# Softmax of k with channels on partitions: maximum by free-axis reductions, subtraction as the bias of the exponential, 32x32 transposes in place

## Chip, cores and metric

The kernel runs on one core of a Trainium2 chip. The metric is the device time of one execution in microseconds (us), as the median of several runs; lower is better. All times below come from the runs, or from one execution that the hardware profiler recorded.

## What is computed

The inputs are eight images (b = 0 to 7) of eight heads, 576 tokens and 64 channels per head. Three blocks follow one another: linear attention, a gated block whose gate mixes tokens, and a gated convolution block.

```python
def _attn_ref(q, k, v):
    q_s = np.exp(q - np.max(q, axis=-1, keepdims=True))        # over channels
    q_s = q_s / (np.sum(q_s, axis=-1, keepdims=True) + 1e-09)
    k_s = np.exp(k - np.max(k, axis=2, keepdims=True))         # over tokens
    k_s = k_s / (np.sum(k_s, axis=2, keepdims=True) + 1e-09)
    kv = np.einsum('bhsd,bhse->bhde', k_s, v)
    return np.einsum('bhsd,bhde->bhse', q_s, kv)
...
    x = attn_out.transpose(0, 2, 1, 3).reshape(B, S, H * D)
    h = gelu_tanh(x @ w_in);  u, v = h[..., :512], h[..., 512:]
    v_s = np.einsum('ts,bsd->btd', w_sg, layernorm(v) * g_ln) + b_sg[None, :, None]
    x = x + (u * v_s) @ w_out
...
    h = np.maximum(x @ w_in2, 0.0)
    return (h * sigmoid(conv3(h, conv_w))) @ w_out2
```

The softmax of k runs over the tokens, separately for each head and channel: 512 maxima per image. Its denominator is not computed apart: v carries a column of ones, so that the matmul of k and v gives the sums too.

## The kernel before

Matmuls are done in three passes of fp32r operands split in a high and a low part (`mm3`, lines 61 to 64). The run has three stretches. Up to about 57 us the inputs land, image 0 goes through attention on a path of its own (functions `s_...`, lines 574 to 653), and the weights begin to be split into high and low parts (`Split`). Then the loop over images (lines 779 to 813) runs attention's remainder and the gated block; it ends near 600 us. The convolution block follows to the end.

In the loop, image b's gated block is a list of 29 groups of matmuls: four `hv` tiles of 128 tokens (and a tile of the leftover tokens of two images), then `hu`, `mx` and `wo` by turns. After each group, `attend` runs steps of other work that `PLAN` (lines 22 to 30) lists by letters: `k` is a step of the k stream, `q` of the q stream, `w` of the weight split, `s` of the mixing matrix's split. The k stream (`k_steps`, line 216) has eleven steps for each of images 1 to 7, and runs one to two images ahead of the gated block.

k of one image arrives with one DMA in the tile `kt`, 128 partitions by 2304. Tokens lie on partitions: block t of 512 columns holds tokens 128t to 128t+127 of all 512 channels; the last 256 columns hold the 64 leftover tokens, heads 0 to 3 on the lower 64 partitions and heads 4 to 7 on the upper ones. The steps are:

- `top`: VectorE takes the maximum over the four blocks and the leftover, down to 128 x 512 in the scratch tile `scr` (lines 221 to 224).
- `spread`: a 32x32 transpose (229), a reduction to 16 numbers per partition (230), exchanges between halves and neighbouring quarters of the partitions (`swap64`, `swap32`, lines 204 to 214), and a transpose that broadcasts the 512 maxima back over the partitions (235).
- `sub`: GpSimd subtracts them in six instructions (241 to 243).
- `ex`: ScalarE takes the exponential of all 2304 columns in one instruction (246).
- `left_max` to `left_tr`: q's 64 leftover tokens.
- `back_kv` twice: 80 small matmuls with 64 columns of `kt` as weights (368, 372), division by the sums, a split; the second then issues the loads of the next k and v. `xt_left` last.

GpSimd executes in the order of the program (`manual_schedule`). The other engines' order is set by a planner as the program is built: an instruction that is earlier in the program goes first among those that its model finds ready. Each engine then executes its own list strictly in order. What stands beside the k steps in those lists: `hv`'s Gelu on ScalarE (428) that frees a PSUM tile, its statistics on VectorE (432 to 436), and between them GpSimd's `pow` (435), a 128 x 1 instruction that `vnh` (444) and `lt` (453) wait for. The matmul groups take PSUM tiles from a pool of four (`mm_tile`). ScalarE loads a table whenever it goes from Gelu to exponential or back; a copy needs none.

Of the kernel before, what the change touches and what calls it, by code (L numbers as in the profile page):

```python
# [8 lines left out]
F32 = mybir.dt.float32  # L9
F32R = mybir.dt.float32r  # L10
U32 = mybir.dt.uint32
AF = mybir.ActivationFunctionType
ALU = mybir.AluOpType
# [23 lines left out]
def attn_gated_conv_kernel(ctx, tc, q, k, v, q0, k0, w_in, g_ln, w_sgT, b_sg, w_out, w_in2, conv_w, w_out2, out):  # L37
# [141 lines left out]
    at = es2.enter_context(tc.tile_pool(name="at", bufs=1, side="right", reuse_waits="tile"))  # L179

    kt = at.tile([128, 2304], F32, name="kt")
    vt = at.tile([128, 18, 2, 65], F32, name="vt")
    ql = [at.tile([128, 512], F32R, name=f"ql{c}") for c in range(4)]
    qlL = at.tile([128, 256], F32R, name="qlL")
# [29 lines left out]
                dve.tensor_copy(dst[32 * i:32 * i + 32], src[32 * j:32 * j + 32])  # L214

    def k_steps(b):
        m, mT, bc = scr[:, 0:512], scr[:, 512:1024], scr[:, 0:512]
        left = kt[:, 2048:2304]

        def top():  # L220
            E[CFG['kt'][min(b - 1, 3)]].tensor_tensor(scr, kt[:, 0:1024], kt[:, 1024:2048], ALU.max)
            dve.tensor_tensor(m, scr[:, 0:512], scr[:, 512:1024], ALU.max)
            dve.tensor_tensor(m[0:64, 0:256], m[0:64, 0:256], left[0:64], ALU.max)
            dve.tensor_tensor(m[64:128, 256:512], m[64:128, 256:512], left[64:128], ALU.max)

        def spread():
            r1 = at.tile([128, 16], F32, tag="r1", name="r1")
            r2 = at.tile([128, 16], F32, tag="r2", name="r2")
            dve.transpose(out=mT, in_=m)
            dve.tensor_reduce(r1, mT.rearrange("p (a b) -> p a b", b=32), axis=AX.X, op=ALU.max)  # L230
            swap64(r2, r1)
            dve.tensor_tensor(r1, r1, r2, ALU.max)
            swap32(r2, r1)
            dve.tensor_tensor(r1, r1, r2, ALU.max)
            dve.transpose(out=bc.rearrange("p (a b) -> p a b", b=32),
                          in_=r1.unsqueeze(2).to_broadcast([128, 16, 32]))

        def sub():
            for t in range(4):
                kc = kt[:, t * 512:t * 512 + 512]  # L240
                pool.tensor_tensor(kc, kc, bc, ALU.subtract)
            pool.tensor_tensor(left[0:64], left[0:64], bc[0:64, 0:256], ALU.subtract)
            pool.tensor_tensor(left[64:128], left[64:128], bc[64:128, 256:512], ALU.subtract)

        def ex():
            act.activation(kt, kt, AF.Exp)

        qv = qt[4].rearrange("p (j a) -> p j a", a=32)
        lm = at.tile([128, 8], F32, tag="lm", name="lm")
        lx = at.tile([128, 8], F32, tag="lx", name="lx")  # L250

        def left_max():
            dve.tensor_reduce(lm, qv, axis=AX.X, op=ALU.max)
            swap32(lx, lm, CFG['sl'][min(b - 1, 2)])
            dve.tensor_tensor(lm, lm, lx, ALU.max)
            pool.tensor_tensor(qv, qv, lm.unsqueeze(2).to_broadcast([128, 8, 32]), ALU.subtract)

        def left_exp():
            act.activation(qv, qv, AF.Exp)
            dve.tensor_reduce(lm, qv, axis=AX.X, op=ALU.add)  # L260

        def left_mul():
            swap32(lx, lm, CFG['sl'][min(b - 1, 2)])
            dve.scalar_tensor_tensor(lm, lm, 1e-9, lx, ALU.add, ALU.add)
            dve.reciprocal(lm, lm)
            pool.tensor_tensor(qv, qv, lm.unsqueeze(2).to_broadcast([128, 8, 32]), ALU.mult)

        def left_tr():
            t = at.tile([128, 256], F32, tag="qTL", name="qTL")
            dve.transpose(out=t, in_=qv.rearrange("p j a -> p (j a)"))  # L270
            qh[4] = at.tile([128, 256], F32R, tag="q4", name="q4")
            act.activation(qh[4], t, AF.Copy)
            dve.tensor_tensor(qlL, t, r32(qh[4]), ALU.subtract)

        return [top, spread, sub, ex, left_max, left_exp, left_mul, left_tr,
                lambda: back_kv(b, 0), lambda: back_kv(b, 1), lambda: xt_left(b)]

    def q_steps(b):
# [80 lines left out]
    def back_kv(b, c2):  # L359
        ps = mm_tile()  # L360
        for i in range(2):
            hp = c2 * 2 + i
            for t in range(5):
                for e in range(2):
                    o = ps[64 * e:64 * e + 64, i * 128:i * 128 + 65]
                    if t < 4:
                        c = t * 512 + hp * 128 + 64 * e
                        pe.matmul(o, kt[:, c:c + 64], vt[:, t * 4 + hp, e], start=(t == 0), stop=False)
                    else:
                        r = slice(0, 64) if hp < 2 else slice(64, 128)  # L370
                        c = 2048 + i * 128 + 64 * e
                        pe.matmul(o, kt[r, c:c + 64], vt[r, 16 + i, e], start=False, stop=True)
        pv = ps[:, 0:256].rearrange("p (c f) -> p c f", c=2)
        rt = at.tile([128, 2], F32, tag=f"rs{c2}", name=f"rs{c2}")
        kvf = scr[:, 512:768].rearrange("p (c f) -> p c f", c=4)
        dve.tensor_scalar(rt, pv[:, :, 64], 1e-9, None, ALU.add)
        dve.reciprocal(rt, rt)
        dve.tensor_tensor(kvf[:, 2 * c2:2 * c2 + 2], pv[:, :, 0:64], rt.unsqueeze(2).to_broadcast([128, 2, 64]), ALU.mult)
        if c2 == 0:
            return  # L380
        for e in range(2):
            r = slice(64 * e, 64 * e + 64)
            act.activation(kv_hi[r, :, r], kvf[r], AF.Copy)
        for e in range(2):
            r = slice(64 * e, 64 * e + 64)
            dve.tensor_tensor(kv_lo[r, :, r], kvf[r], r32(kv_hi[r, :, r]), ALU.subtract)
        if b + 1 < B:
            load_k(b + 1)
            load_v(b + 1)
# [192 lines left out]
    def s_kt(hp):  # L582
        ps = mm_tile()
        for t in range(4):
            o = hp * S + t * 128
            pe.transpose(ps[:, t * 128:t * 128 + 128], k0t[:, o:o + 128], ident)
        act.activation(kt[:, 0:2048].rearrange("p (t f) -> p t f", t=4)[:, :, hp * 128:hp * 128 + 128],
                       ps.rearrange("p (t f) -> p t f", t=4), AF.Copy)

    def s_ktl():  # L590
        ps = mm_tile()
# [347 lines left out]
def _layouts(i):  # L939
    import numpy as np  # L940

    def token_major(a):
        a = a.transpose(0, 2, 1, 3).reshape(-1, S, DM)
        main = a[:, :512].reshape(-1, 4, 128, DM).transpose(0, 2, 1, 3).reshape(-1, 128, 2048)
        left = a[:, 512:].reshape(-1, 64, 2, 256).transpose(0, 2, 1, 3).reshape(-1, 128, 256)
        return np.concatenate([main, left], axis=2)
# [4 lines left out]
    k0 = i["k"][0].transpose(0, 2, 1).reshape(4, 128, S).transpose(1, 0, 2)  # L951
    k0 = k0.reshape(128, 4 * S)
    conv = i["moe2_conv_w"].reshape(3, NFC, 128).transpose(2, 0, 1).reshape(128, 3 * NFC)
    r = {
        "q": q,
        "k": token_major(i["k"]),
        "v": token_major(i["v"]).reshape(B, 128, 18, 2, 64),
        "q0": token_major(i["q"][0:1])[0],
        "k0": k0,
# [28 lines left out]
```

## Time and profile before

| | |
|---|---|
| median of 3 runs | 1017.7 us (1016.02 to 1017.9) |
| span of the profiled execution, first to last instruction | 1016.5 us |
| TensorE (matmul) busy | 942.5 us, 93% |
| VectorE busy | 777.1 us, 76%, 1414 instructions |
| ScalarE busy | 459.6 us, 45%, 902 instructions |
| GpSimd busy | 433.5 us, 43%, 526 instructions |
| mean granted TensorE clock | 0.966 of full speed |

The time of the profiled execution itself is not given apart from its span; the median of the runs is 1.2 us above the span. In the rows, PE is TensorE, PEld its weight loads, DVE VectorE, ACT ScalarE, POOL GpSimd. A busy time counts instructions, not how well they use the engine; consecutive instructions of DVE and ACT overlap a little, so a sum of durations is slightly more than the time that passes. In a timeline, what stands in brackets is how long the engine had been idle and whose result it then waited for.

### The profile page before, as it was taken

The page shows a single profiled execution, that of the slowest core. Times are in us where ns is not written, and L with a number is a line of the kernel's source. Part 1 is how long each engine was busy: PE and PEld are TensorE (multiplying, and loading weights), DVE is VectorE, ACT ScalarE, POOL GpSimd, SP SyncE. Part 2 cuts the span into 40 slices and gives each one's busy share as a digit, 9 for nine tenths or more (in the row PEclk, how much of TensorE's full clock was granted, in tenths as well). Part 3 has the DMA queues.
Part 4 walks back from the last instruction along what each step waited for, and adds up shares of the span by engine and source line. Part 5 has one row for each costly group of instructions (what it writes and reads, how often), then busy time and mean ns, then how long its engine had stood idle before and what let it go on. Part 6 is the DMA issues. An engine that isn't in the chain of part 4 may idle for free.

```text
span 1016.5 us, 16164 instructions
## 1 busy us (share of the span) xinstructions
PE 942.5 (93%) x6144; PEld 851.9 (84%) x6144; DVE 777.1 (76%) x1414; ACT 459.6 (45%) x902; POOL 433.5 (43%) x526
## 2 busy tenths in 40 slices
PE   4777988999999999999988989799999999999998
PEld 3566968879889899898977989699999999989996
DVE  8999896898687777967898598977476757675663
ACT  6554635455546246463534245434343434343332
POOL 6378736556744376556576286611011101110000
PEclk9687997999999999999999998899999999999999
DMA  7721322151143212310222242112011201010001
GB/s 239 231 86 42 106 81 73 48 167 32 50 117 111 67 32 74 104 41 29 84 84 89 75 149 88 47 43 75 25 48 42 88 12 54 36 43 11 14 28 52
DMA packets 34564, 74.10 MB, mean 73 GB/s; under 512 B 3508, under 2 KB 14772, under 8 KB 32696
## 3 DMA queue, kind: packets, MB, share of 16 engines
q1 hardware_dynamic: 34488, 73.09, 22.8%
q8 instruction: 48, 0.79, 0.3%
q14 instruction: 28, 0.23, 0.1%
HBM read 54.20 MB, written 18.87 MB: 72 GB/s over the span
## 4 chain that ended last, share of the span: by engine, by line
PE 44%; DVE 10%; POOL 2%; ACT 2%; issue 2%; DMA 1%; POOLq 0%; DVEq 0%; ACTq 0%
PE mm L62 8%; PE mm L64 8%; PE mm L63 8%; PE acc L63 6%; PE acc L62 6%; PE acc L64 6%; DVE t L100 1%; DVE t L106 1%; DVE t L99 1%; POOL s L110 1%; DVE gl L498 1%; DVE x2s L519 1%; DVE s L109 1%; DMA s<-in_w_out 1%; ACT s L101 0%
## 5 line engine op out<-in xcount | busy, mean ns | idle before, releaser
L62 PE MATMUL mm<-xh,w2h 128*128 128x288 f32 x512 | 153.0, 299 | 3.9 <-ACT h L843 3.9
L64 PE MATMUL mm<-xh,w2l 128*128 128x288 f32 x512 | 152.6, 298 | 0.0
L63 PE MATMUL mm<-xl,w2h 128*128 128x288 f32 x512 | 152.4, 298 | 0.0
L62 PE MATMUL acc<-wAh,yh 128*128 128x512 f32 x256 | 101.5, 396 | 5.3 <-ACT yh L855 5.3
L62 PEld LDWEIGHTS mm<-xh,w2h 128*128 128x128 f32 x512 | 97.7, 191 | 7.2 <-ACT h L843 4.5
L63 PE MATMUL acc<-wAl,yh 128*128 128x512 f32 x256 | 101.9, 398 | 0.0
L63 PEld LDWEIGHTS mm<-xl,w2h 128*128 128x128 f32 x512 | 97.7, 191 | 2.5
L64 PE MATMUL acc<-wAh,yl 128*128 128x512 f32 x256 | 98.7, 395 | 0.0
L64 PEld LDWEIGHTS mm<-xh,w2l 128*128 128x128 f32 x512 | 97.8, 191 | 0.1
L853 ACT ACTIVATE cv<-cv 128x576 f32<-128x576 f32 x64 | 43.9, 685 | 115.9 <-DVE cv L847 115.8
L856 DVE TENSOR_TENSOR yl<-cv,yh 128x576 fp32r<-128x576 f32 x64 | 51.9, 811 | 52.4 <-ACT yh L855 52.4
L843 ACT ACTIVATE h<-mm 128x288 f32<-128x288 f32 x128 | 52.3, 411 | 80.4 <-PE mm L64 80.4
L62 PE MATMUL mm<-xh,wAh 128*128 128x288 f32 x256 | 78.0, 305 | 7.5 <-DVE u L493 4.0
L64 PE MATMUL mm<-sgh,vnl 128*128 128x288 f32 x256 | 77.2, 303 | 5.2 <-DVE rd L434 3.2
L62 PE MATMUL mm<-sgh,vnh 128*128 128x288 f32 x256 | 78.1, 306 | 3.9 <-ACT u L479 2.4
L520 POOL TENSOR_TENSOR x2s<-x2s,xl 128x288 f32<-128x288 f32 x64 | 55.6, 897 | 60.5 <-DVE x2s L519 48.1
L854 DVE TENSOR_TENSOR cv<-cv,h 128x576 f32<-128x576 f32 x64 | 48.8, 764 | 41.5 <-ACT cv L853 40.8
L63 PE MATMUL acc<-gl,wouth 128*128 128x288 f32 x256 | 73.4, 301 | 5.6 <-DVE gl L498 5.6
L64 PE MATMUL mm<-xh,wAl 128*128 128x288 f32 x256 | 77.6, 303 | 0.8 <-POOL wAl L119 0.7
L63 PE MATMUL mm<-xl,wAh 128*128 128x288 f32 x256 | 77.3, 302 | 0.0
L63 PE MATMUL mm<-sgl,vnh 128*128 128x288 f32 x256 | 77.0, 301 | 0.0
L295 POOL TENSOR_TENSOR q<-q,qm 128x512 f32<-128x512 f32 x56 | 61.1, 1121 | 36.1 <-PE mm L64 14.8
(245 smaller groups left out, 2728.4 us busy)
## 6 DMA issues: line engine op xcount, KB each, us to landing
vt<-in_v SPq DMA_DIRECT2D x8, 1152.0 KB, 10.1
x2d<-x2s SPq DMA_DIRECT2D x16, 576.0 KB, 3.3
out<-ot SPq DMA_DIRECT2D x32, 256.0 KB, 2.1
kt<-in_k SPq DMA_DIRECT2D x7, 1152.0 KB, 5.2
xf<-x2d SPq DMA_DIRECT2D x7, 1152.0 KB, 5.6
q<-in_q SPq DMA_DIRECT2D x28, 256.0 KB, 2.6
s<-in_w_in SPq DMA_DIRECT2D x16, 256.0 KB, 2.9
s<-in_w_out SPq DMA_DIRECT2D x16, 256.0 KB, 2.6
```

Source lines behind the costliest of these rows:

```text
L62: pe.matmul(ps, ah, bh, start=start, stop=False)
L63: pe.matmul(ps, ah, bl, start=False, stop=False)
L64: pe.matmul(ps, al, bh, start=False, stop=stop)
L99: dve.tensor_scalar(a.bitcast(U32), h, 3, 0x3FFFFFF8, ALU.logical_shift_left, ALU.bitwise_and)
L100: dve.scalar_tensor_tensor(a.bitcast(U32), h, 0xC0000000, a.bitcast(U32), ALU.bitwise_and, ALU.bitwise_or)
L106: dve.scalar_tensor_tensor(a, hf, GUARD * GUARD, a, ALU.is_ge, ALU.mult)
L295: pool.tensor_tensor(q3[c], q3[c], qm[:, cols(c)].unsqueeze(2).to_broadcast([128, 16, 32]), op)
L520: (dve if CFG['x2'][min(b, 2)] == 'd' else pool).tensor_tensor(x2s[:, m], x2s[:, m], r32(x_lo[b][:, m, cs]), ALU.add)
L843: act.activation(h[:, 1 + hf * HALF:1 + hf * HALF + HALF], ps, AF.Relu)
L853: act.activation(cv, cv, AF.Sigmoid)
L854: dve.tensor_tensor(cv, cv, h[:, 1:S + 1], ALU.mult)
L856: dve.tensor_tensor(yl, cv, r32(yh), ALU.subtract)
```

## The change

k arrives in another layout. Instead of tokens, 32 channels lie on a group of 32 partitions: partition 32g + r holds channel r (of the lower or upper half of a head's 64) for token quarter g of each block of 128, and the free axis runs over head, block, channel half and the quarter's 32 tokens. So each row of the tile belongs to one channel of a head, up to the four groups of partitions.

- `top` becomes four reductions of 128 x 512 and one of 128 x 256, with negated maxima.
- `spread` keeps the exchanges, now with minima, loses both transposes and the 512-wide reduction, gains two small minima with the leftover's, two ScalarE copies of 64 x 8, and one GpSimd addition of 128 x 256 (the leftover's subtraction).
- `sub` is gone; `ex` becomes 16 exponentials of 128 columns (four runs of 32), each with a bias read per partition, and one of 256.
- A new step `turn` transposes `kt` in place in 32x32 blocks: five VectorE instructions. After it tokens lie on partitions as before.
- The number of steps stays eleven; `PLAN` is unchanged. `back_kv` reads its weights at other columns, and `s_kt`, which writes image 0's k, makes two copies per head pair where it made one.

```diff
     def k_steps(b):
-        m, mT, bc = scr[:, 0:512], scr[:, 512:1024], scr[:, 0:512]
-        left = kt[:, 2048:2304]
+        k4 = kt[:, 0:2048].rearrange("p (h t e r) -> p h e t r", h=8, t=4, e=2)
+        left = kt[:, 2048:2304].rearrange("p (g r) -> p g r", r=32)
...
         def top():
-            E[CFG['kt'][min(b - 1, 3)]].tensor_tensor(scr, kt[:, 0:1024], kt[:, 1024:2048], ALU.max)
-            dve.tensor_tensor(m, scr[:, 0:512], scr[:, 512:1024], ALU.max)
-            dve.tensor_tensor(m[0:64, 0:256], m[0:64, 0:256], left[0:64], ALU.max)
-            dve.tensor_tensor(m[64:128, 256:512], m[64:128, 256:512], left[64:128], ALU.max)
+            for i in range(4):
+                dve.tensor_reduce(r1[:, 4 * i:4 * i + 4].rearrange("p (h e) -> p h e", h=2), k4[:, 2 * i:2 * i + 2],
+                                  axis=AX.XY, op=ALU.max, negate=True)
+            dve.tensor_reduce(lb, left, axis=AX.X, op=ALU.max, negate=True)
 
         def spread():
-            r1 = at.tile([128, 16], F32, tag="r1", name="r1")
-            r2 = at.tile([128, 16], F32, tag="r2", name="r2")
-            dve.transpose(out=mT, in_=m)
-            dve.tensor_reduce(r1, mT.rearrange("p (a b) -> p a b", b=32), axis=AX.X, op=ALU.max)
+            for e in range(2):
+                r = slice(64 * e, 64 * e + 64)
+                dve.tensor_tensor(r1[r, 8 * e:8 * e + 8], r1[r, 8 * e:8 * e + 8], lb[r], ALU.min)
             swap64(r2, r1)
-            dve.tensor_tensor(r1, r1, r2, ALU.max)
+            dve.tensor_tensor(r1, r1, r2, ALU.min)
             swap32(r2, r1)
-            dve.tensor_tensor(r1, r1, r2, ALU.max)
-            dve.transpose(out=bc.rearrange("p (a b) -> p a b", b=32),
-                          in_=r1.unsqueeze(2).to_broadcast([128, 16, 32]))
-
-        def sub():
+            dve.tensor_tensor(r1, r1, r2, ALU.min)
+            for e in range(2):
+                r = slice(64 * e, 64 * e + 64)
+                act.activation(lb[r], r1[r, 8 * e:8 * e + 8], AF.Copy)
+            pool.tensor_tensor(left, left, lb.unsqueeze(2).to_broadcast([128, 8, 32]), ALU.add)
+
+        def ex():
+            for g in range(16):
+                kg = k4[:, g // 2, g % 2]
+                act.activation(kg, kg, AF.Exp, bias=r1[:, g:g + 1])
+            act.activation(kt[:, 2048:2304], kt[:, 2048:2304], AF.Exp)
+
+        def turn():
             for t in range(4):
                 kc = kt[:, t * 512:t * 512 + 512]
-                pool.tensor_tensor(kc, kc, bc, ALU.subtract)
-            pool.tensor_tensor(left[0:64], left[0:64], bc[0:64, 0:256], ALU.subtract)
-            pool.tensor_tensor(left[64:128], left[64:128], bc[64:128, 256:512], ALU.subtract)
-
-        def ex():
-            act.activation(kt, kt, AF.Exp)
+                dve.transpose(out=kc, in_=kc)
+            dve.transpose(out=kt[:, 2048:2304], in_=kt[:, 2048:2304])
...
-        return [top, spread, sub, ex, left_max, left_exp, left_mul, left_tr,
+        return [top, spread, ex, turn, left_max, left_exp, left_mul, left_tr,
...
-                        c = t * 512 + hp * 128 + 64 * e
+                        c = (hp * 2 + e) * 256 + t * 64
...
-        act.activation(kt[:, 0:2048].rearrange("p (t f) -> p t f", t=4)[:, :, hp * 128:hp * 128 + 128],
-                       ps.rearrange("p (t f) -> p t f", t=4), AF.Copy)
+        for e in range(2):
+            act.activation(ktv[:, hp * 2 + e], ps.rearrange("p (t e d) -> p e t d", t=4, e=2)[:, e], AF.Copy)
```

## Rows read from the trace of the kernel before

**Rows 1.** Busy time per engine in stretches: stretch, length, busy (instructions), granted clock, DMA.

```profile
core 0: us, PE busy (x) PEld busy (x) DVE busy (x) ACT busy (x) POOL busy (x), PEclk, DMA share, GB/s
57.00:94.00 37.00, 22.95 (x105) 19.25 (x105) 36.75 (x45) 18.06 (x32) 29.60 (x22) 0.77 0.25 73
...
115.00:220.00 105.00, 94.59 (x709) 83.41 (x705) 89.58 (x189) 49.03 (x94) 62.66 (x62) 0.95 0.37 107
220.00:480.00 260.00, 254.38 (x1882) 234.54 (x1882) 202.39 (x438) 126.40 (x244) 147.28 (x144) 1.00 0.23 67
...
165.00:180.00 15.00, 14.02 (x112) 13.06 (x108) 12.48 (x33) 6.69 (x14) 5.65 (x6) 0.66 0.54 153
```

**Rows 2.** Timeline of TensorE, where it had been idle: start, duration, instruction, idle time.

```profile
93.10 0.61 PE L62 MATMUL mm<-xh,wAh 128*128 128x288 f32 x1 [2.99 <-DVE u L493]
...
163.73 0.69 PE L368 MATMUL mm<-vt,kt 128*64 128x65 f32 x16 [2.25 <-ACT kt L246]
167.78 1.13 PE L368 MATMUL mm<-vt,kt 128*64 128x65 f32 x16 [0.98 <-DVE u L493]
```

**Rows 3.** Sums over images 1 to 7: instructions on `scr`, then on `kt`.

```profile
sum 103.00, PE 0.00 PEld 0.00 DVE 42.31 ACT 0.00 POOL 0.00; mean PE 0.00 PEld 0.00 DVE 6.04 ACT 0.00 POOL 0.00
...
sum 81.00, PE 1.15 PEld 1.08 DVE 0.00 ACT 14.91 POOL 53.67; mean PE 0.16 PEld 0.15 DVE 0.00 ACT 2.13 POOL 7.67
```

**Rows 4.** VectorE by line and shape: count, busy us, mean ns of one.

```profile
L290 DVE TENSOR_REDUCE qm<-q 128x16 f32<-128x512 f32 x56 | 37.5, 675 | 13.6 <-ACT q L304 11.0 <-DMA q<-in_q 2.5
L316 DVE STREAM_TRANSPOSE qT<-q 128x512 f32<-128x512 f32 x28 | 19.5, 698 | 6.6 <-POOL q L295 3.9 <-POOL ql L320 2.6
...
L270 DVE STREAM_TRANSPOSE qTL<-q 128x256 f32<-128x256 f32 x7 | 3.1, 439 | 2.1 <-POOL q L266 1.9
L260 DVE TENSOR_REDUCE lm<-q 128x8 f32<-128x256 f32 x7 | 2.9, 413 | 6.0 <-ACT q L259 6.0
```

**Rows 5.** GpSimd by line and shape.

```profile
L241 POOL TENSOR_TENSOR kt<-kt,scr 128x512 f32<-128x512 f32 x28 | 40.8, 1488 | 7.4 <-issue 7.4
...
L256 POOL TENSOR_TENSOR q<-q,lm 128x256 f32<-128x256 f32 x7 | 5.0, 712 | 0.0
```

**Rows 6.** ScalarE by line and shape.

```profile
L212 ACT ACTIVATE lx<-lm 32x8 f32<-32x8 f32 x48 | 9.9, 206 | 6.2 <-DVE lm L253 4.0 <-DVE lm L260 1.4
...
L246 ACT ACT_TABLE_LOAD x7 | 9.0, 1283 | 0.1
...
L259 ACT ACTIVATE q<-q 128x256 f32<-128x256 f32 x7 | 2.9, 410 | 0.7 <-POOL q L256 0.6
```

**Rows 7.** Timeline of ScalarE: exponentials with a bias at the start, table loads later.

```profile
7.32 0.35 ACT L578 ACTIVATE scr<-k0t,sm 128x64 f32<-128x64 f32 x1
7.58 0.71 ACT L580 ACTIVATE k0t<-k0t,sm 128x512 f32<-128x512 f32 x1
8.19 0.62 ACT L599 ACTIVATE q0t<-q0t 128x512 f32<-128x512 f32 x1
...
107.02 1.28 ACT L479 ACT_TABLE_LOAD   x1
...
109.04 1.28 ACT L259 ACT_TABLE_LOAD   x1
```

**Rows 8.** Timelines of VectorE and GpSimd around the subtraction for image 2.

```profile
148.75 1.48 DVE L445 SCALAR_TENSOR_TENSOR vnl<-v,rd,vnh 128x512 fp32r<-128x512 f32 x2 [0.47 <-ACT vnh L444]
...
153.72 3.45 DVE L445 SCALAR_TENSOR_TENSOR vnl<-v,rd,vnh 128x512 fp32r<-128x512 f32 x2 [0.47 <-ACT vnh L444]
...
158.03 0.15 DVE L434 TENSOR_SCALAR rd<-mv 128x1 f32<-128x1 f32 x1
...
164.46 0.83 DVE L455 SCALAR_TENSOR_TENSOR lt<-v,rd,lt 64x512 fp32r<-64x512 f32 x1 [5.58 <-ACT lt L453]
...
153.62 6.41 POOL L241 TENSOR_TENSOR kt<-kt,scr 128x512 f32<-128x512 f32 x4
...
161.60 0.55 POOL L435 TENSOR_TENSOR rd<-rd,nhalf 128x1 f32<-128x1 f32 x1
```

More of the change, by code (lines that the diff above doesn't have):

```diff
@@ L181, in attn_gated_conv_kernel @@
     kt = at.tile([128, 2304], F32, name="kt")
+    ktv = kt[:, 0:2048].rearrange("p (h t d) -> p h t d", t=4, d=64)
     vt = at.tile([128, 18, 2, 65], F32, name="vt")
@@ L216, in k_steps @@
     def k_steps(b):
-        m, mT, bc = scr[:, 0:512], scr[:, 512:1024], scr[:, 0:512]
-        left = kt[:, 2048:2304]
+        k4 = kt[:, 0:2048].rearrange("p (h t e r) -> p h e t r", h=8, t=4, e=2)
+        left = kt[:, 2048:2304].rearrange("p (g r) -> p g r", r=32)
+        r1 = at.tile([128, 16], F32, tag="r1", name="r1")
+        r2 = at.tile([128, 16], F32, tag="r2", name="r2")
+        lb = at.tile([128, 8], F32, tag="lb", name="lb")
         def top():
-            E[CFG['kt'][min(b - 1, 3)]].tensor_tensor(scr, kt[:, 0:1024], kt[:, 1024:2048], ALU.max)
-            dve.tensor_tensor(m, scr[:, 0:512], scr[:, 512:1024], ALU.max)
-            dve.tensor_tensor(m[0:64, 0:256], m[0:64, 0:256], left[0:64], ALU.max)
-            dve.tensor_tensor(m[64:128, 256:512], m[64:128, 256:512], left[64:128], ALU.max)
+            for i in range(4):
+                dve.tensor_reduce(r1[:, 4 * i:4 * i + 4].rearrange("p (h e) -> p h e", h=2), k4[:, 2 * i:2 * i + 2],
+                                  axis=AX.XY, op=ALU.max, negate=True)
+            dve.tensor_reduce(lb, left, axis=AX.X, op=ALU.max, negate=True)
@@ L953, in _layouts @@
     conv = i["moe2_conv_w"].reshape(3, NFC, 128).transpose(2, 0, 1).reshape(128, 3 * NFC)
+    k = i["k"][:, :, :512].reshape(B, H, 4, 4, 32, 2, 32).transpose(0, 3, 6, 1, 2, 5, 4).reshape(B, 128, 2048)
+    kl = i["k"][:, :, 512:].reshape(B, 2, 4, 2, 32, 2, 32).transpose(0, 1, 3, 6, 2, 5, 4).reshape(B, 128, 256)
     r = {
         "q": q,
-        "k": token_major(i["k"]),
+        "k": np.concatenate([k, kl], axis=2),
         "v": token_major(i["v"]).reshape(B, 128, 18, 2, 64),
```

## The prediction

> **What bounds the kernel now.** I read the busy times by stretch first, then the places where TensorE idles, then what ends those idles, and only then the instructions that the change touches. The last of k's steps ends before 480 us, so nothing behind that can gain or lose except by a shift of the start. The stretches differ [rows 1]. From 57 to 94 us (image 0's gated block) VectorE is busy 36.75 of 37 us: it is the bound, and TensorE stands idle for 37 - 22.95 = 14.1 us, at a mean clock of 0.77. The idle at 93.10 us, 2.99 us long, ends with VectorE's product of gate and mixture [rows 2]. From 115 to 220 us VectorE is busy 89.58 of 105 us, and TensorE idles 10.4 us. From 220 to 480 us TensorE is busy 254.38 of 260 us: there it is the bound itself, and no relief of another engine can bring more than 5.6 us. So the change can pay only before 220 us, and what it costs can show everywhere.
>
> One idle hangs on k directly: at 163.73 us TensorE had waited 2.25 us for the exponential of image 2's k, and four us later 0.98 us more for VectorE [rows 2]. The chain behind it is GpSimd's. Its six subtractions began at 153.62 us; the `pow` of the leftover tile, whose input VectorE had finished at about 158.2 us, could start only behind them at 161.60 us, so that VectorE idled 5.58 us for the `lt` copies that follow [rows 8]. After these idles the granted clock from 165 to 180 us is 0.66, a mix of the two levels, 2.4 and 1.2 GHz: 15 x 0.34 = 5.1 us worth of full clock is missing [rows 1].
>
> **The change, part by part.**
>
> *VectorE.* All k instructions that disappear write `scr` (two that read it into `r` included): 42.31 us for seven images, 6.04 us each [rows 3]. Added per image: four reductions of 128 x 512 at 0.675 us = 2.70, one of 128 x 256 at 0.41, four transposes at 0.698 = 2.79, one of 128 x 256 at 0.44 [rows 4], and two small minima at about 0.15, the price of the 128 x 1 instruction at 158.03 us [rows 8]: 6.64 us. The exchanges stay. That is 0.6 us more per image, 4.2 in all. Against it, GpSimd's subtractions slow VectorE's two-input instructions beside them: two `vnl` took 1.48 us together ahead of the subtraction and 3.45 us under it [rows 8]. The relief lies between nothing and 2.0 us per image; I take 1.0, so VectorE ends up 2.8 us lighter in all (between 4.2 heavier and 9.6 lighter).
>
> *GpSimd.* 53.67 us of subtraction go [rows 3], seven additions of 128 x 256 at 0.71 us come [rows 5]: 48.7 us less. The one addition now stands a step earlier in GpSimd's fixed order, and waits for VectorE's exchanges and two ScalarE copies; queued behind it are `pow` and q's instructions. In the row of image 2 the exchanges would have been done ten us before, so I cost this wait at nothing, and at up to 3.4 us per image (what `pow` loses now, 158.2 to 161.60 us [rows 8]) where the exchanges are late.
>
> *ScalarE.* With a bias, the 64-column exponential starts 0.26 us ahead of the next instruction and the 512-column one 0.61 us [rows 7], so a column costs 0.35 / 448 = 0.78 ns, and 128 columns take 0.26 + 0.05 = 0.31 us. Sixteen are 5.0 us, the last one of 256 columns 0.41, and two copies 0.21 each [rows 6]: 5.8 us against 2.13 [rows 3]. That is 3.7 us more per image, 26 us in all, on an engine that is busy 49 of 105 and 126 of 260 us [rows 1]; the cover is its idle time, and if that is in the wrong place the price is the second slower rival below.
>
> *The chain from the maxima to the weights.* Before: 7.67 us on GpSimd and 2.13 on ScalarE [rows 3], 9.8 us. After: 5.4 us of exponentials, with the transposes following block by block and 0.70 + 0.44 us left over behind the last one: 6.5 us. The reductions write no `scr`, so `top` of one image no longer waits until `back_kv` of the one before has read it. DMAs are the same in number and size. `back_kv` has the same 80 matmuls.
>
> *Start.* Each of four 512-column copies into `kt` becomes two of 256. By the bias rows that is 2 x 0.41 against 0.61, at most 0.8 us in all, at least nothing; I take 0.4.
>
> **The sum**, by stretch. Up to 57 us: +0.4. From 57 to 94 us: the transposes of image 1 (3.2 us) may fall into the full VectorE, or behind it; the subtraction's pressure (2.0) is gone. Between +3.2 and -2.0; both sides weigh about the same and I take 0. From 115 to 220 us: the idles of 2.25 and 0.98 us go, for `pow` no longer queues behind 7.7 us and the exponential no longer waits for GpSimd; next late is VectorE's own product, so not more than that. The clock gives back between 0 and 5.1 us; I take 0.5, since other idles in this stretch stay. Together -3.7, between -8.3 and, if a new wait stands in the old one's place, +1. From 220 to 480 us: 0, between -2 and what the slower rivals say. Sum: -3.3. The profiled span of 1016.5 us becomes 1013.2; the median of the runs is 1.2 us above the span, so 1014.4 us. All low ends give -12.3, that is 1005.4.
>
> **The rivals.**
>
> *No change (1016 to 1019.5).* TensorE's idles come back elsewhere, because the planner orders three engines anew, or the 3.2 us are filled by VectorE's extra 0.6 us per image. For it: only 3.2 us of idle name k's chain at all. Against it: GpSimd loses a ninth of its work and `pow` its longest obstacle.
>
> *Slower, by VectorE waiting for ScalarE.* Before, no VectorE instruction of k needs an exponential; now five do, and VectorE's list is fixed. What stands behind them, the statistics of `hv` and the products for `wo`, is what TensorE waits for. q shows the price of such a handover: VectorE idled 11.0 us for q's exponentials over seven images [rows 4], 1.6 each. With the 0.6 us of extra work that is 2.2 us for each of images 1 to 3, whose time is VectorE's; later ones are covered. Then +6.6 + 0.4 and no gain: 1024.7 us. It decides if the transposes stand in the list at a point that ScalarE reaches later than planned.
>
> *Slower, by Gelu between the exponentials.* One long instruction could not be divided; seventeen can, and each Gelu in between costs two table loads of 1.28 us [rows 6], as at 107.02 and 109.04 us, where Gelus went between two exponentials [rows 7]. ScalarE is then taken for 1.28 + 5.4 + 2.6 = 9.3 us. TensorE can go on for four PSUM tiles: 12 matmuls at 254.38 / 1882 = 0.135 us each [rows 1] are 1.6 us a tile, 6.5 us of cover. So 2.8 us are lost per divided image; with three of seven divided +8.4 - 3.3 gives 1022.8 us. It decides from the point at which Gelu's tile is not the newest of the four. The Trainium skill, page ScalarE: Activation LUTs, section What ACT_TABLE_LOAD costs, speaks against dividing: it puts a switch at about 2.66 us, a drain of 1.38 us beside the load. By that figure, an estimate, a divided image would lose 2.8 us more, and three of them would give about 1031 us. The trace doesn't show that drain: the load at 107.02 us takes 1.28 us, and the next load two Gelus later starts at 109.04 us.
>
> *A larger gain (1005 to 1010).* The clock from 165 to 180 us comes back whole and VectorE's relief reaches the stretch of 57 to 94 us.
>
> **Chances.** The forecast, 1010 to 1015.6, gets 0.40: the chain gets shorter by rows. The larger gain 0.12, because it needs the clock as well. No change 0.20. VectorE's wait 0.15, the divided exponentials 0.13: each needs the planner to place work badly, which the rows can't exclude. What a measurement can tell from no change is about 0.2%, 2 us. Faster is 0.52, within 0.2% 0.20, slower 0.28. The range, 1005 to 1025, leaves out about a tenth on the slow side and less on the fast one.
>
> **What would show it.** GpSimd busy should fall from 433.5 to about 385 us, ScalarE's rise by some 26 us or, with its overlaps counted twice, a little more. At `pow` of image 1's leftover tile no wait behind k's work; at image 2's `back_kv` no idle of TensorE above half a us. The table loads for the exponential of k should stay at seven or so: ten or more with Gelus between is the divided rival. A wait of VectorE's transposes for k's exponentials of over 1 us per image is the other. If GpSimd falls as said, neither wait appears and the time still stands, the gain was hidden and the first rival holds. The prediction is wrong in its first step if TensorE's idle between 220 and 480 us grows past 8 us.

## The result and the profile after

The changed kernel takes 1027.9 us as the median of its runs (1026.46 to 1029.12) against 1017.8 us for the kernel before: a ratio of 1.0104, with a 95% interval of 1.0087 to 1.0121. One execution of the kernel before fell into a slower state (1050.3 us), and the ratio leaves it out. By the ratio the change is slower by about 1.0%, 10.6 us. Forecast were 1014.4 us and a range that ended at 1025; the time went the other way and lies outside the range.

The page's first part, kernel after: busy time and instructions of each engine over a span of 1025.1 us.

```profile
PE 944.3 (92%) x6144; PEld 855.6 (83%) x6144; DVE 766.4 (75%) x1449; ACT 511.5 (50%) x1054; POOL 374.9 (37%) x491
```

The stretches of [rows 1], kernel after, columns as there:

```profile
57.00:94.00 37.00, 23.72 (x104) 20.07 (x105) 36.05 (x49) 18.15 (x34) 27.91 (x22) 0.73 0.24 74
115.00:220.00 105.00, 95.79 (x729) 85.73 (x728) 84.97 (x210) 66.18 (x143) 48.29 (x52) 0.95 0.38 108
220.00:480.00 260.00, 248.01 (x1819) 229.45 (x1818) 186.08 (x428) 149.62 (x311) 106.95 (x114) 0.97 0.22 65
...
165.00:180.00 15.00, 13.61 (x120) 12.29 (x117) 11.48 (x34) 8.41 (x15) 6.61 (x6) 0.66 0.40 123
```

VectorE and GpSimd lost work, as intended: 777.1 to 766.4 and 433.5 to 374.9 us. ScalarE gained 52 us, twice the forecast. From 57 to 94 us and from 115 to 220 us TensorE was busy slightly longer than before, by 0.8 and 1.2 us. From 220 to 480 us, where nothing could be gained but much lost, it stands idle for 260 - 248.0 = 12.0 us instead of 5.6, and the granted clock falls from 1.00 to 0.97.

Where in that stretch? A fixed event of each image tells: the store of half an image of the gated block's result. Timeline of SyncE's queue, kernel before, at the ends of images 2, 3 and 4 and at the first half of image 5 (the second store of the last row is its end); then the same, kernel after:

```profile
288.06 0.51 SPq L521 DMA_DIRECT2D x2d<-x2s  x1
...
349.63 0.52 SPq L521 DMA_DIRECT2D x2d<-x2s  x1
...
413.47 0.52 SPq L521 DMA_DIRECT2D x2d<-x2s  x1
454.97 14.98 SPq L521 DMA_DIRECT2D x2d<-x2s  x2
```

```profile
285.22 0.52 SPq L528 DMA_DIRECT2D x2d<-x2s  x1
...
356.15 0.52 SPq L528 DMA_DIRECT2D x2d<-x2s  x1
...
416.78 0.52 SPq L528 DMA_DIRECT2D x2d<-x2s  x1
466.01 0.53 SPq L528 DMA_DIRECT2D x2d<-x2s  x1
```

The changed kernel is 2.8 us ahead at the end of image 2 (forecast 3.3). It loses 9.4 us during image 3, gets 3.2 back during image 4, loses 7.7 in the first half of image 5, and nothing afterwards. In both losses TensorE stops while ScalarE is at k's exponentials. Timelines of ScalarE and TensorE, kernel after, during image 3:

```profile
290.38 1.28 ACT L246 ACT_TABLE_LOAD   x1
291.67 4.80 ACT L246 ACTIVATE kt<-kt,r 128x128 f32<-128x128 f32 x16
296.49 1.28 ACT L435 ACT_TABLE_LOAD   x1
297.79 0.60 ACT L435 ACTIVATE v<-mm 128x512 f32<-128x512 f32 x1
...
298.44 0.46 PE L62 MATMUL mm<-xh,wAh 128*128 128x288 f32 x1 [2.46 <-ACT v L435]
```

```profile
285.00:298.00 13.00, 10.98 (x58) 9.23 (x56) 9.68 (x27) 9.27 (x24) 3.42 (x4) 1.00 0.27 77
298.00:302.00 4.00, 3.56 (x15) 3.57 (x16) 3.22 (x8) 3.74 (x10) 1.57 (x2) 0.58 0.01 2
```

From the first table load to the next Gelu 7.41 us pass, and the Gelu is what hands TensorE a free PSUM tile: TensorE has stopped for 2.46 us when it comes. Behind that idle the granted clock of the next 4 us (second fence, columns of [rows 1]) is 0.58, near the lower of the two levels, 1.2 GHz. So this wait is paid a second time in slower matmuls. In image 5 TensorE idles 2.47 us up to 429.98 and, three matmuls later, 2.30 us up to 433.24 us, and the clock is 0.61 for the next 6.8 us. There the load comes at 422.98 and the next Gelu only at 432.78 us, 9.80 us later, because ScalarE also does other work between the exponentials (two `vnh`, a copy `xLh`, four small copies). The first of the two idles ends with VectorE's `xLl`, which needs that `xLh` (at 428.70 us on ScalarE, behind 13 of the exponentials); the second ends with the Gelu.

Waits of the first 500 us, kernel after (engine, line, what was waited for: total us, times, longest):

```profile
PE mm L62 <- ACT u L486: 7.3, 6, 2.3
...
PE mm L62 <- ACT v L435: 6.5, 4, 3.4
...
DVE kt L252 <- ACT kt L246: 11.8, 14, 2.8
```

The first two are Gelus, 13.8 us of TensorE's waiting; in the kernel before they are 4.0 us (`u` 2.3, `v` 1.7). The third is VectorE's, the one that the first slower rival spoke of.

The lines of k, kernel after, that answer to [rows 3 to 6]:

```profile
L226 DVE TENSOR_REDUCE r<-kt 128x4 f32<-128x512 f32 x28 | 17.2, 674 | 0.5 <-DMA kt<-in_k 0.5
L252 DVE STREAM_TRANSPOSE kt<-kt 128x512 f32<-128x512 f32 x28 | 19.8, 707 | 12.1 <-ACT kt L246 11.8
...
L241 POOL TENSOR_TENSOR kt<-kt,lb 128x256 f32<-128x256 f32 x7 | 5.0, 718 | 6.2 <-ACT lb L240 6.2
...
L246 ACT ACTIVATE kt<-kt,r 128x128 f32<-128x128 f32 x112 | 34.0, 388 | 0.1
...
L486 ACT ACT_TABLE_LOAD x18 | 23.1, 1283 | 3.8 <-DVE gl L505 3.0 <-DVE rs L383 0.6
L246 ACT ACT_TABLE_LOAD x5 | 6.4, 1283 | 0.1
L247 ACT ACT_TABLE_LOAD x6 | 7.7, 1283 | 0.1
```

Table loads are 49 in all, 27 before: at 1.28 us each 28 us of the 52 that ScalarE gained. The leftover's exponential (L247), one instruction behind GpSimd's addition, has a load of its own in six of seven images.

### The profile page after: what moved, and what is told of

It is laid out like the page before. It is cut to its first block, busy times and chain, and to the rows that moved or that the text cites. A ratio compares the mean times of both kernels' runs of the same rounds, so it can differ in the third digit from the quotient of the medians.

```text
span 1025.1 us, 16297 instructions
## 1 busy us (share of the span) xinstructions
PE 944.3 (92%) x6144; PEld 855.6 (83%) x6144; DVE 766.4 (75%) x1449; ACT 511.5 (50%) x1054; POOL 374.9 (37%) x491
## 4 chain that ended last, share of the span: by engine, by line
PE 45%; DVE 9%; ACT 2%; issue 2%; POOL 1%; DMA 1%; ACTq 0%; POOLq 0%; DVEq 0%
PE mm L62 9%; PE mm L64 9%; PE mm L63 9%; PE acc L63 6%; PE acc L62 6%; PE acc L64 6%; DVE t L106 1%; DVE t L100 1%; DVE t L99 1%; DVE x2s L526 1%; DVE s L109 1%; DVE gl L505 0%; DVE cv L853 0%; DVE cv L852 0%; ACT s L101 0%
## 5 line engine op out<-in xcount | busy, mean ns | idle before, releaser
L62 PE MATMUL mm<-xh,wAh 128*128 128x288 f32 x256 | 80.3, 313 | 16.3 <-ACT u L486 8.2
L863 DVE TENSOR_TENSOR yl<-cv,yh 128x576 fp32r<-128x576 f32 x64 | 51.9, 811 | 51.6 <-ACT yh L862 51.4
L527 POOL TENSOR_TENSOR x2s<-x2s,xl 128x288 f32<-128x288 f32 x64 | 51.8, 840 | 75.1 <-DVE x2s L526 56.2
L63 PE MATMUL acc<-gl,wouth 128*128 128x288 f32 x256 | 75.6, 306 | 3.5 <-DVE gl L505 3.4
```

Source lines behind the costliest of these rows:

```text
L62: pe.matmul(ps, ah, bh, start=start, stop=False)
L63: pe.matmul(ps, ah, bl, start=False, stop=False)
L527: (dve if CFG['x2'][min(b, 2)] == 'd' else pool).tensor_tensor(x2s[:, m], x2s[:, m], r32(x_lo[b][:, m, cs]), ALU.add)
L863: dve.tensor_tensor(yl, cv, r32(yh), ALU.subtract)
```

## Experiments

Three theories. A: ScalarE's turn for k, 17 exponentials and their loads instead of one, takes the time that Gelu needs. B: VectorE waits for the exponentials with its transposes. C: the exponentials, freed from GpSimd's order, moved to a place where Gelus are dense. Ratios are to the kernel before, run in the same series.

**The change with one exponential of k instead of 17** (no bias, so the 2048 columns stay unshifted):

```diff
-            for g in range(16):
-                kg = k4[:, g // 2, g % 2]
-                act.activation(kg, kg, AF.Exp, bias=r1[:, g:g + 1])
-            act.activation(kt[:, 2048:2304], kt[:, 2048:2304], AF.Exp)
+            act.activation(kt, kt, AF.Exp)
```

> The changed kernel with one exponential of 2304 columns without bias in place of the 17: the subtraction of the maxima is left out of it for the first 2048 columns (reductions, exchanges, the leftover's addition and the transposes stay). ScalarE loses about 3.3 us per image. Theory A (ScalarE's 17 exponentials and their table loads hold back Gelu, and with it the PSUM tiles): at most 1020 us. Theory B (VectorE's transposes wait for the exponentials; 11.8 us of such waits in the changed kernel): the wait is still there, only shorter, 1022 to 1026. Theory C (k's exponential no longer waits in GpSimd's order and runs amid hv's Gelus, whatever its length): it is still free of GpSimd but for the leftover, 1022 to 1028.

Measured: 1017.4 us, ratio 1.0004 [0.9993, 1.0015], 35 table loads. All 10 us come back. The one exponential also takes in the leftover, so all of it now waits for GpSimd's addition. It was 9.4 us ahead at the end of image 4 and lost 8.5 in the first half of image 5, where the undivided exponential too stood between two loads and another load pair followed. TensorE's waiting for Gelus in the first 500 us is not shorter here: 14.1 us, against 13.8 in the change. What this kernel gains is there by the end of image 2 (10.0 us ahead of the kernel before, the change 2.8), so the sum of those waits does not by itself give the time.

**The division alone, in the kernel before** (`zb` is a new tile of zeros, filled once by GpSimd):

```diff
...
-            act.activation(kt, kt, AF.Exp)
+            for g in range(16):
+                act.activation(kt[:, g * 128:g * 128 + 128], kt[:, g * 128:g * 128 + 128], AF.Exp, bias=zb[:, g:g + 1])
+            act.activation(kt[:, 2048:2304], kt[:, 2048:2304], AF.Exp)
```

> The kernel before with only its one exponential divided: 16 of 128 columns with a bias (of zeros) and one of 256. GpSimd's subtractions stay ahead of it. Theory A: ScalarE's extra 3.3 us per image and the divided table loads alone make it slower, 1023 to 1029. Theories B and C: no transposes behind it, and it still stands behind GpSimd's subtractions, so 1017 to 1020.

Measured: 1031.0 us, ratio 1.0148 [1.0126, 1.0170], 43 loads. Nothing of k's layout or of VectorE's and GpSimd's work on it differs, and the division costs more than the whole change.

**The change without its transposes** (`turn` empty):

> The changed kernel without its transposes (so its k has the wrong layout for the matmul; the work left out is five VectorE instructions per image, 3.2 us). Theory B: the loss goes, 1016 to 1020. Theory A: VectorE is 22 us lighter, but Gelu is still behind the exponentials: 1022 to 1027. Theory C: the same, 1022 to 1028.

Measured: 1025.7 us, ratio 1.0092 [1.0072, 1.0112]. With 23 us of VectorE's work and every wait of it for k's exponentials gone, the gain is 1 to 2 us. B is no cause of weight.

**The leftover's addition on VectorE instead of GpSimd** (`pool` to `dve` in that line):

> The changed kernel with the leftover's addition on VectorE in place of GpSimd, so that the leftover's exponential can directly follow the other 16: no own pair of table loads. Theory A: ten table loads of 1.28 us fewer, 1020 to 1025. Theory B: 0.4 us more per image on VectorE, 1027 to 1030. Theory C: the main burst is where it was, 1025 to 1029.

Measured: 1032.1 us, ratio 1.0159 [1.0136, 1.0183], with ten loads fewer than the change (39). The leftover's lone exponential is gone from the list, and the time is worse: TensorE now waits 4.86 us at once for a Gelu, at 241 us. There a Gelu `v` went in behind the fourteenth exponential, at 233.73 us, and the Gelu `u` that TensorE needed came only at 240.64, behind three more exponentials, other work and the loads. So the number of loads doesn't measure the damage; at this place it is the order of ScalarE's work.

**ScalarE's time alone, in the kernel before** (16 copies of 128 columns ahead of its one exponential; copies need no table):

```diff
+            for g in range(16):
+                act.activation(kt[:, g * 128:g * 128 + 128], kt[:, g * 128:g * 128 + 128], AF.Copy)
             act.activation(kt, kt, AF.Exp)
```

> The kernel before with 16 ScalarE copies of 128 columns of k onto themselves ahead of its one undivided exponential. A copy needs no table: the table loads stay 27 (43 in the kernel that only divides the exponential), while ScalarE gets about 4.5 us more per image, at least as much as the division costs. Theory A1 (the added time of many short instructions is the price): 1025 to 1032 us. Theory A2 (it is the table loads that come with the division, each pair 2.6 us between Gelus): 1017 to 1021 us.

Measured: 1022.9 us, ratio 1.0071 [1.0047, 1.0096], with 27 loads as before. ScalarE is busy 22.1 us longer, and a third of that appears in the time although no load was added: more than theory A2 has and less than A1. The copies stand ahead of the exponential, so they lengthen k's own chain too: from 115 to 480 us TensorE waits 4.1 us for k's exponential, 2.4 in the kernel before.

**One shift for all columns of a partition**: the maxima are reduced to one number per partition, so that one exponential with one bias does, and GpSimd has nothing to do for k. (The division by the sums cancels any shift that a channel's tokens share; a channel whose maximum lies far below the shift loses range.)

```diff
...
-            pool.tensor_tensor(left, left, lb.unsqueeze(2).to_broadcast([128, 8, 32]), ALU.add)
+            dve.tensor_reduce(lb[:, 0:1], r1[:, 0:5], axis=AX.X, op=ALU.min)
...
+            act.activation(kt, kt, AF.Exp, bias=lb[:, 0:1])
```

> The changed kernel with one shift for a partition in place of one for every channel of every head (the maximum over the heads and both halves too, which the division by the sums cancels as well): five reductions into one column, exchanges of one column, one exponential of 2304 columns with a bias, no GpSimd instruction, then the transposes. Theory A: ScalarE's time as in the kernel before, so no slower than before, 1007 to 1019. Theory C (the exponential, no longer behind GpSimd, meets hv's Gelus): image 5 loses some 8 us as in the kernel with one exponential without bias, 1015 to 1022.

Measured: **1004.7 us, ratio 0.9882 [0.9857, 0.9907]**: faster than both kernels, and below either forecast. Windows, this kernel, from 220 to 480 us, and around its exponential in image 5's stretch, then ScalarE there:

```profile
220.00:480.00 260.00, 257.82 (x1923) 239.42 (x1922) 197.94 (x452) 137.06 (x259) 118.03 (x122) 1.00 0.23 68
...
403.00:418.00 15.00, 14.75 (x94) 13.22 (x94) 12.77 (x30) 12.54 (x23) 4.87 (x6) 1.00 0.16 45
```

```profile
403.09 1.28 ACT L237 ACT_TABLE_LOAD   x1
404.38 2.22 ACT L237 ACTIVATE kt<-kt,lb 128x2304 f32<-128x2304 f32 x1
406.62 1.28 ACT L425 ACT_TABLE_LOAD   x1
407.92 0.60 ACT L425 ACTIVATE v<-mm 128x512 f32<-128x512 f32 x1
```

Here 4.83 us pass from load to Gelu, not 7.41, and at this place TensorE does not stop: busy 14.75 of 15 us, at a clock of 1.00.

**The exponentials held back behind GpSimd**, as the subtraction held them before: in the change the 16 biases, in the kernel above the one shift, are copied by GpSimd in the old place of `sub` (the transposes then follow in the step of the exponentials, which is the fourth in place of the third; the leftover's addition moves behind the copy).

```diff
...
+        def hold():
+            pool.tensor_copy(rb, r1)
...
-                act.activation(kg, kg, AF.Exp, bias=r1[:, g:g + 1])
+                act.activation(kg, kg, AF.Exp, bias=rb[:, g:g + 1])
```

> The changed kernel with its 16 biases copied by GpSimd, in the step where the kernel before has its subtractions, and the transposes in the step of the exponentials: the exponentials can't start ahead of GpSimd's turn. 39 table loads, not 49. Theory C: near the kernel before, 1016 to 1021. Theory A: still 17 exponentials, 1022 to 1029.

> The kernel with one shift for a partition, with that shift copied by GpSimd in the step where the kernel before has its subtractions, and the transposes in the step of the exponential. 37 table loads against 39 without the hold. Theory C: the loss in image 5 goes, 1006 to 1012. Theory A: about as without the hold, 1008 to 1018.

Measured: 1028.5 us, ratio 1.0114 [1.0091, 1.0138], no better than the change; and 1017.5 us, ratio 1.0008 [0.9993, 1.0023], which gives back the whole gain of one shift. Holding the exponentials behind GpSimd helps in neither kernel, so C in this form falls. The second run also shows how much hangs on the place: a copy of one column per image and one step later for the exponential, and TensorE waits 2.06 and 2.97 us for Gelus at 426 and 430 us. Timelines of ScalarE and TensorE, one shift held back:

```profile
421.25 1.28 ACT L240 ACT_TABLE_LOAD   x1
...
426.07 0.41 ACT L477 ACTIVATE u<-mm 128x288 f32<-128x288 f32 x1
...
426.54 0.50 PE L62 MATMUL mm<-q,kvh 128*128 128x512 f32 x1 [2.06 <-ACT u L477]
```

From load to Gelu it is 4.82 us, as long as at 403 us without the hold, where TensorE did not stop.

**The dose.** In the kernel with one shift, the exponential is divided in five or in seventeen with the same bias; nothing else differs.

```diff
-            act.activation(kt, kt, AF.Exp, bias=lb[:, 0:1])
+            for g in range(4):
+                act.activation(kt[:, g * 512:g * 512 + 512], kt[:, g * 512:g * 512 + 512], AF.Exp, bias=lb[:, 0:1])
+            act.activation(kt[:, 2048:2304], kt[:, 2048:2304], AF.Exp, bias=lb[:, 0:1])
```

> The dose: the same exponential divided in four of 512 columns and one of 256. ScalarE's turn grows by 4 x 0.25 us, a third of what seventeen add. Theory A by time: a third of the 10 us, so 1007 to 1009. If it is the places between instructions, where another table set can come in, that cost: four places instead of sixteen, but the first one costs as much as the last: 1010 to 1015. Rival (division does not matter): 1003 to 1007.

> The kernel with one shift per partition and one exponential of 2304 columns took 1004.7 us, with 39 table loads. Here that exponential is divided as the change divides it: sixteen of 128 columns and one of 256, all with the same bias; nothing else differs, and nothing is left out. Theory A (ScalarE's longer turn, 5.2 instead of 2.1 us per image, holds back the Gelus that free TensorE's PSUM tiles): 1004.7 and the 10 us that the change and the kernel with one exponential differ by, up to the 13 us that the division cost in the kernel before, so 1015 to 1018. Rival: it was not the division but where the transposes and exchanges stand: 1003 to 1007. If the time rises with the number of table loads staying near 39, it is ScalarE's time and not the loads.

Measured: 1010.1 us, ratio 0.9922 [0.9902, 0.9941], and 1018.8 us, ratio 1.0016 [1.0003, 1.0030]; 39 loads in all three kernels. By ratios that is +4 and +13.6 us on the 1004.7. ScalarE's turn, without the loads, grows from 2.2 to about 3.0 and 5.2 us per image, 6 and 21 us over seven images. Five did not settle whether length or the places between count: 1010.1 us lies at the lower end of the one forecast (1010 to 1015), and 4 us by ratio, 1008.8, inside the other (1007 to 1009). The traces tell more. During image 3 k's exponentials lie alike in the three kernels, with no Gelu between them: from their load to the next Gelu it is 4.83 us (one, at 280.59 us), 5.57 (five, at 279.17) and 7.81 (seventeen, at 282.95), and TensorE stops for a Gelu only at the last, 2.15 us. So length counts, but not in proportion, and the loss of five lies elsewhere. Timelines of ScalarE and TensorE, five exponentials, image 5's:

```profile
403.51 1.28 ACT L238 ACT_TABLE_LOAD   x1
404.81 0.73 ACT L238 ACTIVATE kt<-kt,lb 128x512 f32<-128x512 f32 x1
405.55 1.28 ACT L427 ACT_TABLE_LOAD   x1
406.85 0.60 ACT L427 ACTIVATE v<-mm 128x512 f32<-128x512 f32 x1
407.46 1.28 ACT L238 ACT_TABLE_LOAD   x1
408.76 1.95 ACT L238 ACTIVATE kt<-kt,lb 128x512 f32<-128x512 f32 x3
...
413.97 1.28 ACT L478 ACT_TABLE_LOAD   x1
415.26 0.41 ACT L478 ACTIVATE u<-mm 128x288 f32<-128x288 f32 x1
...
415.73 0.79 PE L62 MATMUL mm<-q,kvh 128*128 128x512 f32 x1 [5.19 <-ACT u L478]
```

A Gelu went in behind the first exponential and cost two more loads, and the next Gelu came 7.8 us later, behind the exponentials, two `vnh` and some copies: TensorE stopped for 5.19 us. Up to the end of image 4 this kernel is level with one shift (table below); it falls back by about 7 us here. In the kernel with seventeen a Gelu goes in behind the first exponential of the same image, at 411.44 us, and TensorE then stops 3.21 and 2.15 us.

**What GpSimd's work for k is worth.** In the kernel before, its six subtractions are left out:

```diff
-            for t in range(4):
-                kc = kt[:, t * 512:t * 512 + 512]
-                pool.tensor_tensor(kc, kc, bc, ALU.subtract)
...
+            pass
```

> The kernel before with GpSimd's six subtractions of k left out (the weights are then taken without the shift); maxima, exchanges and the broadcast stay, the exponential is one instruction. It asks what GpSimd's 54 us and the chain through it are worth in the old layout. If the relief is what carries the gain of the kernel with one shift (13 us): 1003 to 1010. If the gain there came from VectorE's shorter work or from the layout: 1013 to 1018, as the prediction of 3 to 4 us has it.

and in the kernel with one shift, eighteen subtractions in a tile of their own are put in:

```diff
...
+            for t in range(18):
+                pool.tensor_tensor(zs, zs, zs, ALU.subtract)
```

> The kernel with one shift (1004.7 us), and eighteen subtractions of 128x128 on GpSimd in a tile that nothing else uses, ahead of the exponential in the order of the steps: GpSimd gets back about 7 us per image, without any wait for k or by k. If GpSimd's time itself is what costs (its own queue, or VectorE beside it): 1009 to 1015. If only the chain through GpSimd cost, which stays away here: 1003 to 1007.

Measured: 1010.4 us, ratio 0.9933 [0.9918, 0.9948], and 1022.0 us, ratio 1.0048 [1.0030, 1.0066]. Taking GpSimd's part away gives 6.8 us, at the edge of the forecast in which the relief carries the gain; putting about as much back costs 17, above what was expected. Over seven images the eighteen took 60.8 us where about 7 each, 49, were meant: in image 1 they took 0.81 us each, 14.5 us in all, and in the other six 0.43. Timeline of GpSimd, this kernel:

```profile
91.05 15.87 POOL L239 TENSOR_TENSOR zs<-zs 128x128 f32<-128x128 f32 x18
106.88 1.04 POOL L110 TENSOR_TENSOR sa<-sa 128x512 f32<-128x512 f32 x1
```

The splitting of the output weights stood behind them, and image 0's first half was already 8 us later than with one shift (122.9 against 115.0 us). ScalarE's order differs too (33 table loads, 39 with one shift). Whether GpSimd's queue or VectorE beside it makes most of the 17 us was not tried apart.

Stores of half images against the kernel before, in us (minus: earlier):

| kernel | image 2, end | 3, end | 4, end | 5, first half |
|---|---|---|---|---|
| the change | -2.8 | +6.5 | +3.3 | +11.0 |
| change, one exponential | -10.0 | -7.2 | -9.4 | -0.9 |
| one shift | -11.9 | -8.3 | -14.1 | -13.2 |
| one shift, in 5 | -13.4 | -11.6 | -13.7 | -5.4 |
| one shift, in 17 | -9.6 | -5.2 | -8.7 | -0.8 |
| before, no subtraction | -8.1 | -7.6 | -8.4 | -7.0 |
| before, 16 copies | +2.7 | +5.6 | +5.6 | +6.7 |
| before, in 17 | +8.8 | +11.3 | +13.6 | +14.7 |

Each row of the table is one execution. The profiled one was 3.4 us faster than the median of its kernel for one shift in 17 and 2.7 faster for the change with one exponential, and 2.1 slower for one shift in 5, so differences of 2 or 3 us between rows say little.

## Why the prediction was wrong

**The step that failed** is ScalarE's: "That is 3.7 us more per image, 26 us in all [...] the cover is its idle time", which stands in the sum at nothing. The size was right: 4.80 / 16 = 0.30 us an exponential (forecast 0.31), and 511.5 - 459.6 = 51.9 us less 28 of loads leaves 24. The cover was not there: the division alone costs 13.6 us on one shift and 15 in the kernel before, and 22 us of copies without any load cost 7. ScalarE was idle for half of the run [rows 1], but idle time is cover only where no Gelu or copy that TensorE needs stands behind the exponentials on ScalarE's list.

**The rival that came** was the third, Gelu between the exponentials, at a chance of 0.13, but on another condition. It was made to depend on a Gelu going in between. In the changed kernel's bursts that cost most, at 290 and 424 us, none does; the sixteen exponentials with their loads, and in the second what else stood between them, were enough. (It did come true in other kernels: with the leftover's addition on VectorE at 234 us, with one shift in five and in seventeen in image 5.) The prediction's own numbers say so: 1.28 + 5.4 + 1.28 = 8.0 us is more than its cover of 6.5, while before it was 1.28 + 2.13 + 1.28 = 4.7. The cover was held against the divided case alone. Measured: 7.41 us from load to Gelu and 2.46 us of idle, since TensorE had gone on for only 5.6 us after the load at 290.38. That 2.46 lies near the 2.8 of the forecast is luck, for that was priced for 9.3 us and a cover of 6.5. Then came the half clock, which the price had left out.

The Trainium skill, page ScalarE: Activation LUTs, section What ACT_TABLE_LOAD costs, had been weighed there: it adds about 1.38 us of drain to each load. The trace differs: the load at 290.38 us is followed by the exponential at 291.67, 1.29 us later, and it begins 0.02 us after the copy ahead of it has ended. The same section has an activation with a bias per partition at 280 ns and 0.833 ns a column, less 93 ns where they follow one another: 0.294 us for 128 columns, an estimate, with which the 0.30 agrees.

Length alone does not decide it either. At 223.10 us, kernel after, 7.40 us from load to Gelu cost TensorE 0.42 us. In the kernel before, during image 3, 9.54 us pass from load to Gelu. Timeline of ScalarE, then the window from this load to this Gelu (columns of [rows 1]):

```profile
306.04 1.28 ACT L246 ACT_TABLE_LOAD   x1
...
315.58 0.41 ACT L479 ACTIVATE u<-mm 128x288 f32<-128x288 f32 x1
```

```profile
306.04:315.58 9.54, 9.54 (x95) 8.72 (x94) 7.42 (x14) 6.31 (x9) 6.51 (x8) 1.00 0.26 74
```

For 2.36 of them ScalarE waits for GpSimd, and TensorE is busy throughout; and with one shift held back 4.8 us were too long. What TensorE has left to do when ScalarE turns to k differs from place to place, so one number for the cover could not hold.

**Table loads.** "Seven or so" for k's exponential became eleven, but the larger part was not foreseen: loads back to Gelu for `u` rose from 10 to 18, and the leftover's lone exponential had its own pair.

**VectorE waiting for ScalarE**: the wait is there, 11.8 us or 1.7 per image, as the rival had it (1.6); its price was not 6.6 us but at most 2 without the transposes. Of the 11.8 us 8.3 lie between 220 and 480 us, where VectorE is busy 186 of 260 us and has slack. The kernel with one shift has the same wait, 8.7 us, and is the fastest of all.

**What was right.** VectorE's part for k: 17.2 + 19.8 + 3.0 + 2.9 + 3.3 = 46.2 us for seven images, forecast 6.64 each, 46.5. Other VectorE work became lighter by 14.6 us, not the 7 taken: the product `gl` alone fell from 50.3 to 42.1 us, and the engine by 10.7 in all, forecast 2.8. (The upper bound there is 14 - 4.2 = 9.8, not 9.6.) GpSimd fell to 374.9, forecast 385. No `pow` waits behind k's work in image 2. The clock from 165 to 180 us stayed at 0.66, as allowed for. But the idle of [rows 2] at `back_kv` of image 2, forecast below half a us, became another one. Timeline of TensorE, then of ScalarE ahead of it, kernel after:

```profile
164.53 0.69 PE L375 MATMUL mm<-vt,kt 128*64 128x65 f32 x16 [1.87 <-ACT u L486]
```

```profile
161.04 1.28 ACT L266 ACT_TABLE_LOAD   x1
162.34 0.42 ACT L266 ACTIVATE q<-q 128x256 f32<-128x256 f32 x1
162.77 1.28 ACT L486 ACT_TABLE_LOAD   x1
164.06 0.41 ACT L486 ACTIVATE u<-mm 128x288 f32<-128x288 f32 x1
```

TensorE no longer waits for k, but for a Gelu that stands behind a lone exponential of q and its two loads. The gain of GpSimd's relief was forecast at 3.3 us; without the subtractions it is 6.8 in the old layout, and with one shift the whole is 12.

**The criterion** "wrong in its first step if TensorE's idle between 220 and 480 us grows past 8 us" is met: 12.0.

What stays open: in all these kernels three engines are ordered anew, and the place of one exponential was worth 12.7 us (one shift, held back). The runs show that the divided exponential is the cause (with one exponential the loss is gone, and dividing it costs 13.6 and 15 us in two other kernels); how the 10 us of this change divide between the length of ScalarE's turn, its loads and its place was not shown. In the kernel before with 17 exponentials half of the loss is there by the end of image 1, and the two largest idles of TensorE between 115 and 480 us are not put down to a Gelu. The later one leads back to ScalarE all the same, the earlier one probably. The one of 3.07 us at 317 us ends with VectorE's `xl`, and VectorE had itself idled 3.51 us for ScalarE's copy `xh`, which stood behind a load and eight exponentials; over the first 500 us VectorE waits 15.8 us for such copies, 3.8 in the kernel before. The one of 3.66 us, at 167.32 us, is put down to GpSimd, but a Gelu behind eight exponentials and two loads had ended only 0.1 us earlier, so that the Gelu is the likelier cause; this is not shown.

## What to carry to other kernels

An engine that is busy half of the time need not have cover where others wait for it at short intervals: at each place compare the piece in which it is away, loads included, with what the waiting engine can still do there. The same 4.8 us from load to Gelu cost nothing at one place and 2 us at another. Before one long instruction is divided for the sake of a bias per column, ask for a coarser bias that keeps it whole; here that turned 1% slower into 1% faster. Work taken from GpSimd was worth more than was forecast (6.8 us by itself); that this comes from what is queued behind it is likely by the timeline at 91 to 107 us, but not shown apart from VectorE's relief.

## What the runs showed of the hardware

After an idle of 2.46 us (298 us, kernel after) and one of 5.19 us (five exponentials) the granted clock of the next 4 to 5 us lay near its lower level, though the matmuls then stood close together. After 2.47 us of idle, at 429.98 us, the next three matmuls of 512 columns took 0.50, 0.39 and 0.40 us (0.39 to 0.40 at 424 us); the ones behind the second idle, at 433.24 us, were slow. Window of the kernel with five exponentials from the first matmul behind its idle:

```profile
415.70:421.00 5.30, 5.27 (x18) 4.79 (x19) 3.33 (x7) 2.50 (x5) 3.09 (x4) 0.50 0.18 53
```

Matmuls of 288 columns took 0.44 us there and 0.29 before the idle. On GpSimd the same 128x128 subtraction took 0.81 us in image 1, where VectorE was busy 13.45 of 16 us, and 0.43 in the other six images, where VectorE was busy 35% to 79% of the time; a cause was not tried.
